# Moving the first output products of a chunk one slot later in a slot-scheduled attention and feed-forward kernel

## The chip, the cores and the metric

The kernel runs on one core of a Trainium2 chip, as one program with one launch. The metric is the time of the whole program on the device in microseconds (us). A core has five engines that run their own instruction queues in order and wait for each other on semaphores: TensorE (PE, matrix products into PSUM; PEld is its weight load), VectorE (DVE), ScalarE (ACT), GpSimd (POOL) and SyncE (SP, which here only issues DMAs).

## The reference

An attention with a 32-wide window on both sides, 512 local and 32 global positions, 8 batches and 8 heads of 64, is followed by a two-layer feed-forward with the activation h·cos(h). Cut to what matters:

```python
s_g = scale * q_g @ k_all.T;  out_g = softmax(s_g) @ v_all          # 32 global rows
s_l = concat(scale * q_l @ k_g.T, where(|i - j| <= 32, scale * q_l @ k_l.T, -1e9))
out_l = softmax(s_l) @ concat(v_g, v_l)                             # 512 local rows
x = concat(out_g, out_l) as (batch * positions, heads * 64)          # 4352 x 512
h = x @ w_in                                                        # 512 -> 2048
out = (h * cos(h)) @ w_out                                          # 2048 -> 512
```

All values are float32. The kernel gets float32 accuracy out of float16 products by splitting each operand in a high and a low part and adding three products (high·high, high·low, low·high).

## The kernel before

**Feed-forward.** The rows of x are worked off in 17 chunks of 256 rows: chunks 0 to 15 are the local rows (two chunks to a batch), chunk 16 holds the global rows of all batches. A chunk `c` has 8 steps `j`, and each step goes through these functions:

- `m1_a` (L877): 24 matmuls make the hidden tile `ph` of two 128-wide slices of the 2048. `ph` has three PSUM buffers.
- `m1_b` (L899, L900): ACT and DVE reduce the argument of the cosine (`u`).
- `m1_c` (L421): ACT takes the sine (`w`).
- `m1_d` (L912, L914, L918, L919): POOL squares `w`, DVE makes the product `gf` and so frees `ph`, ACT rounds it to `gh`, POOL makes the rest `gl`.
- `m2_a` (L933 to L935): 12 matmuls add the step to the two output tiles `po` of the chunk, six to each. `po` has two PSUM buffers, so the first `m2_a` of a chunk must wait until both tiles of the chunk before are read out.
- `m2_b` (L941, L943), after the last step: ACT reads out `po` 0 and DVE `po` 1, as tiles `o`; `m2_c` stores them.

**Attention.** Two chunks after a batch's turn its x must be ready. Each batch has four pairs of heads. For a pair: SP loads `qkr` (L432, one buffer), DVE takes its maximum `qm` (L472), makes a diagonal `d_qk` (L448), a small PE product `pm_qk` (L454) spreads the maximum over the partitions, ACT and DVE scale and split (`qa` L511, `kl` L512), PE makes four score tiles `ps` (L579, L580), DVE adds the mask and finds row minima (`t`, `mn`, L596), ACT takes the exponentials (L421), ACT and DVE write them as float16 `planes` (L673, L676), SP transposes these by DMA (L688, four for a pair) and PE multiplies with the values (`acc`, L721). Sine and exponential lie in different ACT tables, and `table_act` keeps their order as written; changing from one to the other costs an `ACT_TABLE_LOAD`.

**What sets the order.** Every call is put into a slot by `at(slot, phase, f, ...)`. Chunk `c`, step `j` has slot `8c + j` for `m1_a`; its `m2_a` lies `lag` = 3 slots later. Inside a slot the phases sort the calls: `m1_c` -9, `m1_d` -8, `m1_a` -5, `m1_b` -4, `m2_a` -3, `m2_b` -2. The slots only give the order in which the calls are written. The tile framework (`schedule_with_timeline_sim`) then simulates the program and puts the instructions of each engine in an order of its own, so a moved call can also change the order of other engines. Once written, that order is fixed: an engine whose next instruction waits does nothing else.

In a steady chunk, two pairs of heads lie beside the eight steps, one in slots 0 to 3 and one in slots 4 to 7.

Of the kernel before, what the change touches and what calls it, by code (L numbers as in the profile page):

```python
# [133 lines left out]
def body(tc, qk, v, wi, wo, mask, out):  # L134
    nc = tc.nc
    lag = 3
# [3 lines left out]
    with ExitStack() as ctx:  # L140
# [821 lines left out]
        def at(slot, phase, f, *a):  # L962
            ev[slot].append((phase, len(ev[slot]), f, a))
# [86 lines left out]
        for b in range(2, B):  # L1050
# [7 lines left out]
        ma, mb, mc, md, m2, ob, oc = (  # L1058
            (PE_, PH, PB, PD, PG2, PH2, PA0),
            (-5, -4, -9, -8, -3, -2, -10),  # L1060
            (-7, -4, -9, -8, -6, -2, -10),
        )[MF]
        for c in range(NC + 1):
            at(NS * c, -11, chunk_scales, c)
            for j in range(NS):
                s = NS * c + j
                if c == 0 and j < JS:
                    for kc in range(NPAIR):
                        at(-5 + kc, PJ, m1_a, c, j, kc)
                else:  # L1070
                    at(s, ma, m1_a, c, j)
                at(s, mb, m1_b, c, j)
                at(s + 1, mc, m1_c, c, j)
                at(s + 1, md, m1_d, c, j)
                at(s + lag, m2, m2_a, c, j)
            for k in range(CT // P):
                at(NS * c + NS - 1 + lag, ob, m2_b, c, k)
                at(NS * c + NS + lag, oc, m2_c, c, k)
# [77 lines left out]
```

## Time and profile before

| what | value |
|---|---|
| median of 3 runs | 1049.87 us (1048.74 to 1050.3) |
| the profiled execution, whole | 1045.26 us |
| its span from first to last instruction | 1043.5 us, mean granted TensorE clock 0.941 |
| PE busy in the span | 879.3 us (84%), 7819 matmuls |
| DVE / ACT / POOL busy | 729.4 (70%) / 707.9 (68%) / 463.1 us (44%) |
| PE idle before `po` L933, put down to DVE `o` L941 | 17.7 us, 11 times |
| PE idle before `ph` L877, put down to DVE `gf` L914 | 31.1 us, 12 times |

The first 250 us hold the weights' loading and splitting and the attention of the first two batches. From there to about 870 us chunks and attention run side by side, and from 870 us on the last chunks run alone. Matmuls are pipelined: each is shown longer than the step to the next one, so a busy PE is not PE at its peak. A wait is put down to the engine whose event came last.

### The profile page before, as it was taken

To read this page: it belongs to the slowest core of one execution; us is meant where nothing else is said; L and a number is where in the kernel's file an instruction comes from. 1 tells how busy PE (TensorE), PEld (TensorE's weight loads), DVE (VectorE), ACT (ScalarE), POOL (GpSimd) and SP (SyncE) were. 2 spreads that over 40 slices of the span, in tenths; PEclk is the share of its full clock that TensorE was granted. 3 is DMA by queue.
4 is the path that set the end of the run, shared out by engine and by line. 5 is a ranking of instruction groups with operands and counts; after the bars stand their busy time and mean duration, and the time that the engine had idled before them with its cause. 6 is when DMAs were issued, how large, how long until landed. Compare 5 with 4: busy or idle time off the path is not lost.

```text
span 1043.5 us, 20761 instructions
## 1 busy us (share of the span) xinstructions
PE 879.3 (84%) x7819; PEld 600.3 (58%) x7819; DVE 729.4 (70%) x1797; ACT 707.9 (68%) x1458; POOL 463.1 (44%) x396
## 2 busy tenths in 40 slices
PE   2133558677999999999899998999889999999996
PEld 1112435455566666666666666666667676666663
DVE  5997598999577777786777777877777766433231
ACT  6676478887378776877677667876777777434342
POOL 4885285957334342434233333333334333444442
PEclk9955679887999999999999999999999999999998
DMA  9869622796464546354553545455555442200000
GB/s 368 213 202 218 179 99 89 157 178 127 115 131 89 130 83 162 86 122 90 155 106 94 116 123 108 111 107 145 106 105 102 110 85 63 46 21 21 1 21 21
DMA packets 181565, 120.18 MB, mean 115 GB/s; under 512 B 159832, under 2 KB 159832, under 8 KB 179416
## 3 DMA queue, kind: packets, MB, share of 16 engines
q1 hardware_dynamic: 181464, 118.85, 47.6%
q8 instruction: 61, 1.00, 0.4%
q14 instruction: 40, 0.33, 0.1%
HBM read 51.81 MB, written 8.91 MB: 58 GB/s over the span
## 4 chain that ended last, share of the span: by engine, by line
DVE 36%; PE 29%; DMA 14%; ACT 11%; issue 6%; POOL 2%; SPq 1%; ACTq 0%; DVEq 0%; POOLq 0%
PE ph L877 12%; DMA qkr<-qk 6%; DVE t L596 5%; DVE planes L676 5%; PE po L933 5%; PE po L935 5%; PE po L934 5%; DVE u L900 4%; DMA vr<-v 3%; DVE gf L914 3%; ACT L421 3%; DVE kl L512 2%; DVE qm L472 2%; PE acc L721 2%; DVE vl L570 2%
## 5 line engine op out<-in xcount | busy, mean ns | idle before, releaser
L877 PE MATMUL ph<-xh,wi_h 128*128 128x256 f16 x1024 | 281.8, 276 | 31.1 <-DVE gf L914 31.1
L877 PE MATMUL ph<-xl,wi_h 128*128 128x256 f16 x1024 | 282.3, 276 | 0.0
L877 PE MATMUL ph<-xh,wi_l 128*128 128x256 f16 x1024 | 282.2, 276 | 0.0
L919 POOL TENSOR_TENSOR gl<-gf,gh 128x512 f16<-128x512 f32 x136 | 165.1, 1218 | 234.0 <-ACT gh L918 233.6
L912 POOL TENSOR_TENSOR w<-w 128x512 f32<-128x512 f32 x136 | 145.6, 1075 | 266.5 <-ACT w L421 254.5
L877 PEld LDWEIGHTS <-wi_h 128*128 128x128 f16 x2176 | 211.6, 99 | 68.1 <-DVE gf L914 18.4
L933 PE MATMUL po<-wo_h,gh 128*128 128x512 f16 x544 | 206.9, 384 | 21.3 <-DVE o L941 17.7
L934 PE MATMUL po<-wo_l,gh 128*128 128x512 f16 x544 | 207.2, 381 | 0.6 <-POOL wo_l L268 0.6
L935 PE MATMUL po<-wo_h,gl 128*128 128x512 f16 x544 | 206.9, 381 | 0.0
L421 ACT ACTIVATE w<-u,ca 128x512 f32<-128x512 f32 x136 | 97.0, 721 | 112.6 <-DVE u L900 112.2
L900 DVE SCALAR_TENSOR_TENSOR u<-u,cm,ph 128x512 f32<-128x512 f32 x136 | 100.0, 742 | 97.1 <-ACT u L899 97.0
L421 ACT ACTIVATE t<-t,mn 128x192 f32<-128x192 f32 (+1 forms) x256 | 117.1, 458 | 59.3 <-DVE mn L596 58.8
L918 ACT CAST gh<-gf 128x512 f16<-128x512 f32 x136 | 83.1, 611 | 78.0 <-DVE gf L914 70.6
L914 DVE SCALAR_TENSOR_TENSOR gf<-w,ph 128x512 f32<-128x512 f32 x136 | 92.5, 681 | 55.2 <-POOL w L912 55.0
L877 PEld LDWEIGHTS <-wi_l 128*128 128x128 f16 x1088 | 107.6, 99 | 15.7 <-issue 2.0
L596 DVE CUSTOM_DVE_ANT_0 t<-ps,msk,al 128x192 f32<-128x192 f32 (+1 forms) x256 | 99.5, 426 | 10.4 <-PE ps L580 10.3
L899 ACT ACTIVATE u<-ph,cm 128x512 f32<-128x512 f32 x136 | 92.1, 677 | 16.5 <-PE ph L877 16.5
L934 PEld LDWEIGHTS <-gh 128*128 128x128 f16 x544 | 53.4, 98 | 69.6 <-issue 21.2
L676 DVE SCALAR_TENSOR_TENSOR planes<-t,sm,planes 128x192 f16<-128x192 f32 (+1 forms) x192 | 83.9, 489 | 10.7 <-ACT planes L673 10.7
L935 PEld LDWEIGHTS <-gl 128*128 128x128 f16 x544 | 53.4, 98 | 64.3 <-issue 1.7
L933 PEld LDWEIGHTS <-gh 128*128 128x128 f16 x544 | 53.2, 98 | 54.0 <-issue 5.3
L421 ACT ACT_TABLE_LOAD x57 | 73.1, 1283 | 1.0
(183 smaller groups left out, 1428.4 us busy)
## 6 DMA issues: line engine op xcount, KB each, us to landing
qkr<-qk SPq DMA_DIRECT2D x29, 608.0 KB, 4.6
vr<-v SPq DMA_DIRECT2D x8, 1280.0 KB, 7.8
kh<-qa SPq DMA_DIRECT2D x62, 152.0 KB, 2.6
out<-o SPq DMA_DIRECT2D x34, 256.0 KB, 2.6
qa<-kl SPq DMA_DIRECT2D x31, 152.0 KB, 3.7
kl<-kl SPq DMA_DIRECT2D x31, 152.0 KB, 4.7
wo_h<-wi SPq DMA_DIRECT2D x4, 1024.0 KB, 7.9
raw_wi<-wi SPq DMA_DIRECT2D x4, 1024.0 KB, 10.7
```

The lines of the kernel that those rows point to most:

```text
L421: ins = nc.scalar.activation(*a, **k).ins
L596: nc.vector.tensor_tensor_reduce(t[:, h], pt[:, h], msk[:, MOFF[i] : MOFF[i] + w], al, 3.0e38, ALU.add, ALU.min, mn[:, h : h + 1],)
L676: nc.vector.scalar_tensor_tensor(lo, t[:, h], r, hi, op0=ALU.mult, op1=ALU.subtract)
L877: nc.tensor.matmul(ph[:, a], w[:, kc, f], x[:, kc, q], start=first and ip == 0, stop=last and ip == 2, skip_group_check=True,)
L899: nc.scalar.activation(u, ph, AF.Identity, bias=m)
L900: nc.vector.scalar_tensor_tensor(u, u, m, ph, op0=ALU.subtract, op1=ALU.subtract)
L912: nc.gpsimd.tensor_tensor(w, w, w, op=ALU.mult)
L914: nc.vector.scalar_tensor_tensor(gf, w, 0.5, st.pop(("ph", c, j)).rearrange("p a b -> p (a b)"), op0=ALU.subtract, op1=ALU.mult,)
L919: nc.gpsimd.tensor_tensor(gl, gf, gh, op=ALU.subtract)
L933: nc.tensor.matmul(po[k], gh[:, q], wo_h[:, f], start=(f == 0), stop=False)
L934: nc.tensor.matmul(po[k], gh[:, q], wo_l[:, f], start=False, stop=False)
L935: nc.tensor.matmul(po[k], gl[:, q], wo_h[:, f], start=False, stop=(f == NJ - 1))
```

## The change

One term is added to the slot of `m2_a`. For all chunks but the first, the products of step 0 move from slot `8c + 3` to slot `8c + 4`, where they stand behind `m1_a` of step 4 and ahead of the products of step 1.

```diff
                 at(s, mb, m1_b, c, j)
                 at(s + 1, mc, m1_c, c, j)
                 at(s + 1, md, m1_d, c, j)
-                at(s + lag, m2, m2_a, c, j)
+
+                at(s + lag + (j == 0 and c > 0), m2, m2_a, c, j)
             for k in range(CT // P):
```

No instruction is added or taken away. Names below carry chunk and step (`ph_3_4`), chunk and tile (`po_3_0`), or batch, pair and tile (`t_3_0_2`).

**PE, the turn to chunk 3, before.** Behind the last product of `ph_3_3` come the first of `po_3_0`:

```order
L877 LDWEIGHTS wi_l_87
L877 MATMUL ph_3_3_3907<-xh_1_2049,wi_l_87 128x256
L933 LDWEIGHTS gh_3_0_3691
L933 MATMUL po_3_0_3936<-wo_h_88,gh_3_0_3691 128x512
L934 LDWEIGHTS gh_3_0_3691
```

**PE, the same place now.** Behind `ph_3_3` come the 36 products of `acc_2_2`, and after them `ps`, `pm_qk` and `ph_3_4`:

```order
L877 LDWEIGHTS wi_l_87
L877 MATMUL ph_3_3_3907<-xh_1_2049,wi_l_87 128x256
L721 LDWEIGHTS vh_2_2_3208
L721 MATMUL acc_2_2_3936<-pt_2_2_3885,vh_2_2_3208 64x128
L721 LDWEIGHTS vh_2_2_3208
```

The twelve products of step 0 now follow the 24 of `ph_3_4`, with those of step 1 right behind them. The same holds for chunks 2 to 13; in chunks 14 to 16, which have no attention beside them, `ph_c_4` goes ahead of the twelve products. Chunk 1 keeps its order.

**DVE, slot 6 of chunk 3, before.** `u_3_6` comes first, then the maximum `qm_3_2` of the next pair, whose `qkr` is being loaded, then the score tile `t_3_0_2`:

```order
L914 SCALAR_TENSOR_TENSOR gf_3_5_4175<-w_3_5_4142,ph_3_5_4116 128x512
L900 SCALAR_TENSOR_TENSOR u_3_6_4204<-u_3_6_4204,cm_2_2809,ph_3_6_4179 128x512
L472 TENSOR_REDUCE qm_3_2_4337<-qkr_3_2_4239 128x1
L596 ISA t_3_0_2_4234,mn_3_0_2_4235<-ps_3_0_2_4222,msk_73,al_3_0_3576 128x224
L596 ISA mn_3_0_2_4235 128x1
```

**DVE, the same place now.** `qm_3_2` and `d_qk3_2` stand ahead of `u_3_6`:

```order
L914 SCALAR_TENSOR_TENSOR gf_3_5_4175<-w_3_5_4142,ph_3_5_4116 128x512
L472 TENSOR_REDUCE qm_3_2_4337<-qkr_3_2_4239 128x1
L448 TENSOR_SCALAR d_qk3_2_4339<-ident_64,qm_3_2_4337 128x128
L900 SCALAR_TENSOR_TENSOR u_3_6_4204<-u_3_6_4204,cm_2_2809,ph_3_6_4179 128x512
L596 ISA t_3_0_2_4234,mn_3_0_2_4235<-ps_3_0_2_4222,msk_73,al_3_0_3576 128x224
```

This happens in chunks 2, 3, 5, 7, 9 and 11. There `u_c_4` also moves ahead of `t_x_0` on DVE and `w_c_4` ahead of `u_c_5` on ACT. In chunks 4, 6, 8 and 10 `u_c_6` stays ahead of `qm`; there `u_c_4` moves ahead of `qa` on ACT and, with `gf_c_3`, ahead of `kl` on DVE, and SP issues the copy `qa<-kl` (L524) behind the pair's four transposes.

**ACT, what stands behind `u_3_6` now.** The sine `w_3_6` needs DVE's `u_3_6`; behind it come the table load, the exponentials of pair (3, 0), `gh_3_6` and `u_3_7`:

```order
L899 ACTIVATE u_3_6_4204<-ph_3_6_4179,cm_2_2809 128x512
L421 ACTIVATE w_3_6_4205<-u_3_6_4204,ca_2_2808 128x512
L421 ACT_TABLE_LOAD
L421 ACTIVATE t_3_0_0_4081,sm_3_0_4355<-t_3_0_0_4081,mn_3_0_0_4082 128x192 x2
L421 ACTIVATE t_3_0_1_4162,sm_3_0_4355<-t_3_0_1_4162,mn_3_0_1_4163 128x224 x2
L421 ACTIVATE t_3_0_2_4234,sm_3_0_4355<-t_3_0_2_4234,mn_3_0_2_4235 128x224 x2
L918 CAST gh_3_6_4242<-gf_3_6_4245 128x512
L899 ACTIVATE u_3_7_4274<-ph_3_7_4249,cm_2_2809 128x512
```

From `w_3_6` on this is also the order of before; only `gh_3_5`, which stood between `u_3_6` and `w_3_6`, has moved ahead of both.

## The prediction

> **What bounds the kernel now.** I read the waits of PE first, since the change moves PE's products, then each engine's load by stage, then the chain of waits and the timeline at one chunk's turn.
>
> ```profile
> PE po L933 <- DVE o L941: 17.1, 10, 2.7
> PE ph L877 <- DVE gf L914: 10.6, 8, 1.5
> DVE qm L472 <- DMA qkr<-qk: 41.5, 19, 3.4
> ...
> 237.00:825.00 588.00, 552.28 (x5162) 379.41 (x5159) 440.41 (x1139) 431.09 (x916) 222.97 (x195) 0.98 0.51 115
> 825.00:1043.50 218.50, 208.76 (x1655) 140.65 (x1654) 88.91 (x187) 108.13 (x201) 85.39 (x77) 0.98 0.16 35
> ```
>
> The first three are waits (us in all, times, longest): PE's from 300 to 835 us, DVE's from 310 to 800 us. The last two are busy times of PE, PEld, DVE, ACT and POOL by stage. In the steady stage PE waits 17.1 us for the read-out `o`, which is what the change aims at, and DVE waits 41.5 us for the loads of `qkr`. PE is fullest by its matmul rows (552 of 588 us), but the chain shows who sets the pace (start, us, what):
>
> ```profile
> 312.44 5.05 DMA qkr<-qk
> 317.52 1.42 DVE qm L472
> 318.94 0.36 DVE t L596
> ...
> 320.07 0.61 DVE gf L914
> ...
> 321.23 0.69 ACT u L899
> 321.94 0.75 DVE u L900
> ```
>
> A load, DVE, ACT and DVE follow each other without PE. Such loops make up nearly all of the chain from 395 to 825 us; PE stands in it only where a long wait has made it late. So **the attention's loop through the `qkr` load, DVE and ACT sets the pace up to 825 us, with PE close behind; from the last wait at 825.21 (below) PE runs without a wait and sets the end.**
>
> [...]
>
> **PE's move.** The turn to chunk 3, on DVE (two rows), then PE (two rows), with the row of `d_qk` between:
>
> ```profile
> 343.24 1.42 DVE L472 TENSOR_REDUCE qm<-qkr 128x1 f32<-128x1216 f32 x1 [1.44 <-DMA qkr<-qk]
> 344.58 0.74 DVE L941 TENSOR_SCALAR o<-po,co 128x512 f32<-128x512 f32 x1
> 345.98 0.28 DVE L448 TENSOR_SCALAR d_qk<-ident,qm 128x128 bf16<-128x128 f32 x1
> 345.37 0.38 PE L933 MATMUL po<-wo_h,gh 128*128 128x512 f16 x1 [2.02 <-DVE o L941]
> 348.39 0.22 PE L454 MATMUL pm_qk<-d_qk,ones 128*128 128x128 bf16 x1
> ```
>
> `o` is late because DVE, in order, waits for the load ahead of `qm`. PE waits until 345.37, does six `po`, 36 `acc` and four `ps`, and reaches `pm_qk` at 348.39, when `d_qk` (ended 346.26) is long there. Now `acc` and `ps` come first and PE stands at `pm_qk`, for the same DVE queue, until about 346.3: **the wait on `o` becomes a wait on `d_qk`.** Behind it come 24 `ph` and 24 `po` where there were 24 and 12. So `ph` comes 348.39 - 346.3 = 2.1 us sooner, and the end of the slot is 2.6 us (twelve `po` at 0.215) less 2.1 us, that is 0.5 us, later. In the steady stage `u_c_4` waits behind ACT's `planes` anyway, and DVE's queue to `d_qk` doesn't depend on the moved products: cost 0. Without that cover it is 0.5 us a turn. Chunk 12's turn is the last and PE's tail follows: +0.5 us.
>
> **What the swap on DVE costs.** Slot 6 of chunk 3: SP, then DVE, then ACT.
>
> ```profile
> 358.09 5.54 SPq L688 DMA_TRANSPOSE pt<-planes  x4
> 363.68 0.57 SPq L432 DMA_DIRECT2D qkr<-qk  x1
> 365.43 0.75 DVE L900 SCALAR_TENSOR_TENSOR u<-u,cm,ph 128x512 f32<-128x512 f32 x1 [0.28 <-ACT u L899]
> 368.82 1.42 DVE L472 TENSOR_REDUCE qm<-qkr 128x1 f32<-128x1216 f32 x1 [2.64 <-DMA qkr<-qk]
> 366.27 0.72 ACT L421 ACTIVATE w<-u,ca 128x512 f32<-128x512 f32 x1 [0.37 <-DVE u L900]
> 367.01 1.28 ACT L421 ACT_TABLE_LOAD   x1
> 371.81 0.62 ACT L918 CAST gh<-gf 128x512 f16<-128x512 f32 x1
> 372.33 0.68 ACT L899 ACTIVATE u<-ph,cm 128x512 f32<-128x512 f32 x1
> ...
> 343.87 0.45 ACT L421 ACTIVATE t<-t,mn 128x192 f32<-128x192 f32 x1
> 346.89 0.62 ACT L918 CAST gh<-gf 128x512 f16<-128x512 f32 x1
> ```
>
> Before, DVE does `u_3_6` at 365.43 and then idles 2.64 us for the load; meanwhile ACT takes the sine, changes tables and runs four exponentials. Now `qm` stands in front, so `u_3_6` waits for the load as well, and behind it on ACT the sine, the table load, six exponentials, `gh_3_6` and `u_3_7`. The load itself comes no sooner: SP issues it at 363.68, when four transposes that began at 358.09 are through, and the first waits for `planes0`, which follows the same work as before.
>
> From the start of `qm` to ACT's `u_3_7` it was 372.33 - 368.82 = 3.51 us. Now: `qm` 1.34 (343.24 to 344.58), `d_qk` 0.28, `u` 0.75, sine 0.74 (366.27 to 367.01), table load 1.30, six exponentials with nothing late 3.02 (343.87 to 346.89), `gh` 0.52 (371.81 to 372.33), in all 7.95 us. The difference is **4.4 us**. Nothing behind it takes this up: `u_3_7`, `t_3_0_3`, the next exponentials and sine follow on each other, and the next load of `qkr` hangs on them. `acc` and `xh` are not later than that. The swap is made in chunks 2, 3, 5, 7, 9 and 11; the last reads alike:
>
> ```profile
> 797.79 1.42 DVE L472 TENSOR_REDUCE qm<-qkr 128x1 f32<-128x1216 f32 x1 [2.63 <-DMA qkr<-qk]
> 801.31 0.68 ACT L899 ACTIVATE u<-ph,cm 128x512 f32<-128x512 f32 x1
> ```
>
> 3.52 us again. Six times 4.4 is **+26.4 us**. The trace doesn't show this order, so the bounds are 0 a turn (the load comes before `u_c_6`) and 5.0 (all of `u`'s delay, from 365.43 to 370.44, passes on); I take 4.4, built from rows.
>
> **What comes back.** At three turns DVE's `t` waited for PE's `ps`, which lay behind `po`:
>
> ```profile
> 296.76 0.42 DVE L596 CUSTOM_DVE_ANT_0 t<-ps,msk,al 128x192 f32<-128x192 f32 x1 [1.81 <-PE ps L580]
> 563.40 0.42 DVE L596 CUSTOM_DVE_ANT_0 t<-ps,msk,al 128x192 f32<-128x192 f32 x1 [1.34 <-PE ps L580]
> 777.78 0.42 DVE L596 CUSTOM_DVE_ANT_0 t<-ps,msk,al 128x192 f32<-128x192 f32 x1 [1.27 <-PE ps L580]
> ```
>
> `ps` now lies ahead of `po`: **-4.4 us**.
>
> **Chunks 4, 6, 8 and 10.** `u_c_4` ahead of `qa` delays ACT by 0.6 us.
>
> ```profile
> 409.97 1.36 SPq L803 DMA_TRANSPOSE ptg<-planes_g  x1
> 412.59 5.49 SPq L688 DMA_TRANSPOSE pt<-planes  x4
> ```
>
> DVE does `u_c_4` and `gf_c_3` while it would wait for `qa`, so `planes0` comes no later, the transposes may start some 0.5 us sooner, and the copy L524, now behind them, uses that up ahead of the `qkr` load. PE's 10.6 us of waits for `gf` mostly go, but PE then stands at `pm_qk`. I take 0, within 0.5 us each; uncovered, the 0.6 us would pass on.
>
> **The clock.** PE's longer idling has a price of its own:
>
> ```profile
> 502.81 0.38 PE L933 MATMUL po<-wo_h,gh 128*128 128x512 f16 x1 [2.21 <-DVE o L941]
> ...
> 558.57 0.38 PE L933 MATMUL po<-wo_h,gh 128*128 128x512 f16 x1 [2.50 <-DVE o L941]
> ...
> 559.46 0.63 PE L933 MATMUL po<-wo_h,gh 128*128 128x512 f16 x1
> 559.89 0.63 PE L934 MATMUL po<-wo_l,gh 128*128 128x512 f16 x1
> ...
> 346.83 1.29 PE acc L721 x36
> ...
> 560.95 1.98 PE acc L721 x36
> ...
> 825.21 0.38 PE L933 MATMUL po<-wo_h,gh 128*128 128x512 f16 x1 [1.07 <-DVE o L941]
> ```
>
> After 2.50 us of idling products follow each other at 0.43 us instead of 0.215, and `acc` takes 1.98 instead of 1.29 us: about 1.7 us lost (five `po` at 0.215, and 0.69). After 2.21 us it isn't seen. With DVE 4.4 us later at chunk 11, PE idles longer than 2.5 us before chunk 12's tail, so it pays 1.7 us once on the path. At earlier turns PE has room, as DVE and ACT come later still.
>
> [...]
>
> **Sum**: 26.4 - 4.4 + 0.5 + 1.7 = +24.2 us. On the profiled execution's 1045.26 us that is 1069.5; that execution is 4.6 us below the median of the runs, 1049.87, to which I add the same: **1074.0 us**.
>
> **Rivals.**
> - *PE is the bound* (matmul rows at 94% speak for it, the chain against): the 17.1 us go, 1032.8 us. Decided by whether PE waits at `pm_qk`. 5%.
> - *The load comes in time.* If `qkr` lands before `u_c_6` is ready (365.4 us at chunk 3), the swap costs nothing: 1049.87 - 4.4 + 0.5 = 1046.0. It would have to land 2.6 us sooner or more (DVE's wait in the row at 368.82); SP's transposes speak against it. 6%. This is the case on the other side.
> - *The stall is taken up*, because PE's `acc` and not ACT held `u_c_7` (the chain runs through `acc` at chunk 3): cost and gains cancel, 1050. Six near-equal distances of 3.5 us speak against it. 4%.
> - *The clock falls on the path at every turn*: at the ten turns from chunk 3 to 12, nine more times 1.7 us, 1089 us. PE's room speaks against it. 5%.
>
> **How the numbers follow.** 80% for the forecast. The range is 1056 to 1086: the low end is half of each stall covered, on the profiled execution's time (1045.3 + 13.2 - 4.4 + 2.2), the high end is the stall at 5.0, no gain back, and three turns at the low clock (1049.9 + 30.0 + 0.5 + 5.1 = 1085.5). That leaves out the first three rivals and the last. Faster by over 0.2% (2.1 us, about what a measurement can tell) 11%, within it 4%, slower 85%.
>
> **What would show it.** Right: PE's wait on `o` gone and a wait of `pm_qk` on `d_qk` in its place; six times about 3.5 us of DVE idling ahead of `qm` directly behind `gf_c_5`; about 8 us from `qm` to `u_c_7` at those six turns and 3.5 at the others; chunk 12's turn 20 us or more later than 825. Wrong: loads that land before `u_c_6`, or turns no further apart than before although DVE stalls.

## The result and the profile after

The changed kernel takes **1072.31 us** (median of 4 runs, 1071.65 to 1073.62) against 1049.3 us for the kernel before (4 runs): ratio 1.0224, 95% interval 1.0203 to 1.0246, so 23.0 us slower. Its profiled execution took 1072.69 us with a span of 1070.9 us. Two executions far off the rest, one of 4433.6 us of qm_last below (with it, the median would be 1036.68 us) and one of 1575.72 us of the kernel before, are left out of the medians and ratios.

The waits of PE from 300 to 855 us in the changed kernel (us in all, times, longest):

```profile
PE pm_qk L454 <- DVE d_qk L448: 24.0, 10, 3.5
PE ph L877 <- ACT xh L745: 7.6, 5, 1.9
PE ps L579 <- DVE mn L596: 3.8, 7, 1.5
```

No wait on `o` is left in this stretch. Ten waits of `pm_qk` stand in its place, and they are longer than what they replace.

The busy times by stage, cut at the turn to chunk 12 (window, us, busy PE, PEld, DVE, ACT and POOL; then granted clock of PE, DMA share and GB/s):

```profile
237.00:850.00 613.00, 560.97 (x5211) 383.22 (x5212) 446.81 (x1145) 430.76 (x918) 224.52 (x196) 0.98 0.49 111
850.00:1070.90 220.90, 209.62 (x1621) 140.38 (x1620) 89.85 (x188) 108.22 (x203) 85.34 (x77) 0.98 0.15 35
```

The steady stage is 25 us longer, the tail 2.4 us. The chain of waits of the changed kernel, at slot 6 of chunk 5 (start, us, what):

```profile
478.51 5.10 DMA qkr<-qk
...
483.64 1.43 DVE qm L472
...
485.09 0.29 DVE d_qk L448
485.38 0.67 DVE u L900
...
486.13 0.72 ACT w L421
486.87 1.28 ACT L421
488.17 0.58 ACT t L421 x3
...
488.96 2.05 ACT t L421 x9
491.01 0.51 ACT gh L918
491.52 0.59 ACT u L899
```

This is the stall that the prediction drew: load, `qm`, `d_qk`, then `u_5_6`, its sine, the table load, the exponentials, `gh` and `u_5_7`, one behind the other.

The time from one turn to the next (between the starts of DVE's `o`) shows where the difference lies. Swapped turns are those of the chunks in which `qm` and `d_qk` went ahead of `u_c_6`:

| chunk | 2 | 3 | 4 | 5 | 6 | 7 | 8 | 9 | 10 | 11 |
|---|---|---|---|---|---|---|---|---|---|---|
| swapped | yes | yes | no | yes | no | yes | no | yes | no | yes |
| before, us | 55.14 | 50.75 | 54.65 | 52.04 | 55.75 | 52.87 | 55.46 | 50.38 | 55.74 | 52.20 |
| changed, us | 57.02 | 55.93 | 54.24 | 56.28 | 56.37 | 56.50 | 54.95 | 55.14 | 56.16 | 56.41 |

The six swapped chunks give +23.9 us, the four others +0.1. The stretch behind chunk 12's turn is 1.8 us longer (220.9 against 219.1), and 1.6 us lie ahead of chunk 2. Together that is the 27.4 us between the two spans. The orders of the two kernels differ only from chunk 2 on, and the first turn comes anywhere from 257.3 to 263.9 us in the traces of all runs, so the 1.6 us belong to the spread between executions.

### The profile page after: what moved, and what is told of

It is laid out like the page before. It is cut to its first block, busy times and chain, and to the rows that moved or that the text cites. A ratio compares the mean times of both kernels' runs of the same rounds, so it can differ in the third digit from the quotient of the medians.

```text
span 1070.9 us, 20771 instructions
## 1 busy us (share of the span) xinstructions
PE 887.6 (83%) x7819; PEld 602.8 (56%) x7819; DVE 736.4 (69%) x1797; ACT 705.0 (66%) x1458; POOL 462.5 (43%) x396
## 4 chain that ended last, share of the span: by engine, by line
DVE 35%; PE 24%; ACT 16%; DMA 12%; issue 8%; POOL 3%; SPq 1%; ACTq 0%; DVEq 0%; POOLq 0%
PE ph L877 10%; DMA qkr<-qk 5%; DVE planes L676 5%; DVE u L900 5%; DVE t L596 4%; ACT t L421 4%; PE po L933 4%; PE po L935 4%; PE po L934 4%; ACT L421 4%; DVE gf L914 2%; DVE kl L512 2%; DMA vr<-v 2%; ACT w L421 2%; ACT u L899 2%
## 5 line engine op out<-in xcount | busy, mean ns | idle before, releaser
L877 PE MATMUL ph<-xh,wi_h 128*128 128x256 f16 x1024 | 286.1, 280 | 28.1 <-DVE gf L914 20.5
L877 PE MATMUL ph<-xl,wi_h 128*128 128x256 f16 x1024 | 286.4, 280 | 1.9 <-DVE xl L746 1.9
L877 PE MATMUL ph<-xh,wi_l 128*128 128x256 f16 x1024 | 286.6, 280 | 0.0
L877 PEld LDWEIGHTS <-wi_h 128*128 128x128 f16 x2176 | 214.6, 100 | 87.1 <-issue 39.7
L676 DVE SCALAR_TENSOR_TENSOR planes<-t,sm,planes 128x192 f16<-128x192 f32 (+1 forms) x192 | 91.7, 532 | 10.8 <-ACT planes L673 10.8
L579 PE MATMUL ps<-kh,qa 128*128 128x192 f16 (+1 forms) x256 | 60.3, 271 | 16.5 <-DVE mn L596 9.6
```

Of the source, the lines that this page charges most:

```text
L676: nc.vector.scalar_tensor_tensor(lo, t[:, h], r, hi, op0=ALU.mult, op1=ALU.subtract)
L877: nc.tensor.matmul(ph[:, a], w[:, kc, f], x[:, kc, q], start=first and ip == 0, stop=last and ip == 2, skip_group_check=True,)
```

## The experiments

Each time is a median beside runs of the kernel before on the same chip (medians 1048.2 to 1048.7 us). Line numbers shift by a few between the kernels.

| run | us | ratio to before, 95% interval |
|---|---|---|
| u_first | 1054.84 | 1.0055 (1.0027 to 1.0083) |
| swap_alone | 1072.77 | 1.0244 (1.0195 to 1.0294) |
| load_early | 1057.44 | 1.0086 (1.0062 to 1.0110) |
| load_early_u_first | 1051.20 | 1.0047 (1.0022 to 1.0073) |
| pe_alone | 1046.81 | 0.9982 (0.9961 to 1.0004) |
| others_alone | 1078.06 | 1.0277 (1.0228 to 1.0326) |
| u4_even | 1047.18 | 0.9988 (0.9969 to 1.0008) |
| w4_odd | 1052.53 | 1.0046 (1.0024 to 1.0069) |
| pe_and_swap | 1074.20 | 1.0254 (1.0229 to 1.0278) |
| qm_last | 1034.32 | 0.9886 (0.9838 to 0.9934) |
| qm_last_pe_moved | 1036.43 | 0.9891 (0.9845 to 0.9938) |
| vm_last_too | 1019.30 | 0.9718 (0.9685 to 0.9750) |

### The swap, undone and alone

**u_first** binds `qm` behind `u_c_6` in the changed kernel:

```diff
+                c = 2 * b - 4 + p // 2
+                if b > 2 and p % 2 == 0 and True:
+                    tc.add_manual_dep(qi, st["ui", c, 6].name, order, reason="u_first")
```

> The changed kernel (1072.31 us) with one thing undone: at the six turns DVE does u_c_6 ahead of qm and d_qk again; PE's, ACT's, POOL's and SP's orders stay those of the changed kernel. Theory (the swap costs 4.4 us at each of six turns, the rest of the change brings 4.4 and costs 0.5 to 2): 1072.3 - 26.4 = 1046 us, between 1043 and 1049, with 3.5 us from qm to ACT's u_c_7 at all turns. Rival (PE's moved products, or the other moves on ACT, DVE and SP, cost the time and the swap only stands beside them): above 1060 us.

1054.84 us: 17.5 us come back, less than expected (the range ended at 1049), and the kernel stays 0.55% above before. Something else in the change costs time once the swap is gone.

**swap_alone** makes the swap in the kernel before (`m1_b2` is the DVE half of `m1_b`, bound behind `d_qk`):

```diff
+            if b > 2 and p % 2 == 0 and 2 * b - 4 + p // 2 in SWAP:
+                at(o["qa"] - 1, PJ + 0.5, qk_a, b, p)
...
+                if c in SWAP and j == 6:
+                    at(s, PJ + 0.6, m1_b2, c, j)
```

> The kernel before (1049.3 us) with the swap alone: at the same six turns qm and d_qk stand ahead of u_c_6 on DVE; PE's, POOL's and SP's orders are those of before, and on ACT only gh_c_6 and u_c_7 change places. Theory: 1049.3 + 6 x 4.4 = 1076 us, between 1069 and 1080; a little above the changed kernel, since PE's waits for ps at three turns stay. Rival (the swap costs only together with PE's move): within 5 us of 1049.

1072.77 us, 24.3 above before and inside the expected range: the swap alone makes nearly all of the loss, without PE's move.

### The load

**load_early** keeps the order of PE, DVE, ACT and POOL of the changed kernel and lets SP issue the load earlier. The swap is bound by hand for this, as in swap_alone; SP's copy L524 goes behind the transposes. The line that moves the load:

```diff
-            at(o["load"], PJ, load_qk, b, p)
+            at(o["load"], PA0 if b > 2 and p % 2 == 0 else PJ, load_qk, b, p)
```

> The changed kernel with the swap kept (the orders of PE, DVE, ACT and POOL are the same), but SP issues the qkr load of every second pair (p 0 and 2 of batches 3 to 7) ahead of the four transposes instead of behind them; the copy L524 goes behind the transposes. The load should land about 5 us sooner, some 366 us at the turn where qm began at 372.54, and DVE should do qm directly behind gf_c_5. Theory (the swap costs because u_c_6 waits for the load): the stall falls from about 3.5 us to 0.5 a turn, so at least 6 x 2.7 = 16 us come back: 1056 us or less, down to about 1040 if the loop through the load gets shorter at the other turns too. Rival (the order on DVE and ACT itself costs 4.4 us, load or not): 1068 to 1072. A second rival (the transposes, now later by the load, hold acc): 1072 or more.

DVE in this kernel, slot 6 of chunk 5:

```profile
474.09 0.69 DVE L929 SCALAR_TENSOR_TENSOR gf<-w,ph 128x512 f32<-128x512 f32 x1 [0.63 <-POOL w L927]
474.70 1.41 DVE L474 TENSOR_REDUCE qm<-qkr 128x1 f32<-128x1216 f32 x1
476.14 0.60 DVE L449 TENSOR_SCALAR d_qk<-ident,qm 128x128 bf16<-128x128 f32 x1
476.67 0.73 DVE L912 SCALAR_TENSOR_TENSOR u<-u,cm,ph 128x512 f32<-128x512 f32 x1
```

`qm` follows `gf_5_5` with no idle time, in the same order that cost 3.1 us of idling here in the changed kernel. The time is 1057.44 us, 1.4 us above the range that was expected: 14.9 us came back, so the order without the late load costs little. What stays is the remainder that u_first showed too.

**load_early_u_first** makes both edits.

> Both edits at once: the load ahead of the transposes, and u_c_6 ahead of qm. Theory: the swap's price is the wait for the load, so beside load_early this gains only 0 to 4 us (the u behind qm and d_qk costs under 0.7 us a turn where the load is there); and if the loop through the load sets the pace up to 825 us, an earlier load makes this one faster than u_first: 1033 to 1044, where PE becomes the bound at about 1033. Rival (the load's place matters only through the swap): the time of u_first, within 2 us.

1051.20 us, 3.6 below u_first. Both expectations failed: the time did not fall towards 1033, and it is not u_first's either. The earlier load took away the waits in the middle of the chunks, but DVE still waits ten times at the turns (16.3 us for `qkr` from 300 to 830 us, 27.2 in u_first). Its longest waits here are those for ACT's `u`: 63.7 us, against 32.1 in the kernel before. So in this order ACT is late too; why, the runs w4_odd and u4_even below look into.

### The two halves of the change

From here on the order of an engine is written out: at the end of the kernel every instruction of that engine is bound behind its forerunner in a list, so that nothing else moves.

```diff
+            for x, y in zip(seq, seq[1:]):
+                tc.add_manual_dep(v[y], v[x].name, order, reason="pin")
```

**pe_alone** takes PE's order from the changed kernel and all other orders from before.

> PE in the order of the changed kernel, every other engine (DVE, ACT, POOL, SP) in the order of before, all written out by hand. By the prediction's steps the PE move itself costs 0.5 us once and frees 4.4 us at the three turns where t waited for ps: 1049 - 3.9 = about 1045 us. Rival (the 0.5 us is not covered and is paid at each of the ten turns, and what is freed is lost again): 1052 to 1056, the time of u_first (1054.8). Second rival (the moves of u_c_4 and w_c_4 on ACT and DVE cost what u_first has over before): 1045 to 1050.

**others_alone** takes PE's order from before and all others from the changed kernel.

> The other half: PE in the order of before, every other engine in the order of the changed kernel. Theory (the time is lost by the orders on DVE and ACT): the swap's 24.3 us as in swap_alone and 3 to 7 us for the moves of u_c_4 and w_c_4, 1074 to 1081 us, at or above the changed kernel. Rival (the loss needs PE's move): 1049 to 1060.

1046.81 and 1078.06 us. PE's move alone is worth -1.9 us (-4.1 to +0.4). The reordering of the other engines, which the scheduler added, is worth +29 us alone; beside it PE's move takes 5.7 us back by the medians (1078.06 to 1072.31; the two intervals overlap). The waits of PE in pe_alone, 300 to 855 us:

```profile
PE pm_qk L457 <- DVE d_qk L451: 18.8, 10, 3.6
PE ph L880 <- DVE gf L917: 8.1, 7, 1.5
PE gps L765 <- DVE gmn L782: 1.2, 3, 0.5
```

PE now waits about as long for `d_qk` as it did for `o` before (18.8 and 17.1 us): the move only renames the wait.

### What else the scheduler moved

**u4_even** puts only the moves in chunks 4, 6, 8 and 10 on top of pe_alone (ACT's part):

```diff
+ACTIVATE u_4_4<-ph_4_4,cm_4 128x512
 ACTIVATE qa_3_3<-qkr_3_3,qs_3_3 128x1216
...
+ACTIVATE w_4_4<-u_4_4,ca_4 128x512
-ACTIVATE u_4_4<-ph_4_4,cm_4 128x512
 CAST gh_4_3<-gf_4_3 128x512
 ACTIVATE u_4_5<-ph_4_5,cm_4 128x512
-ACTIVATE w_4_4<-u_4_4,ca_4 128x512
```

> pe_alone (1046.8 us) with the changed kernel's orders on DVE, ACT, POOL and SP in chunks 4, 6, 8 and 10 only: u_c_4 ahead of qa on ACT, u_c_4 and gf_c_3 behind kl on DVE, the copy L524 behind the transposes. The prediction took these for 0. Theory (u_c_4's 0.57 us on ACT delays qa and nothing covers it, with up to as much again behind it): 4 x 0.6 to 4 x 1.1, so 1049 to 1051 us. Rival (covered, as predicted): within 1.5 us of 1046.8.

**w4_odd** puts only those in chunks 2, 3, 5, 7, 9 and 11 on top, without the swap (ACT's part):

```diff
+ACTIVATE w_5_4<-u_5_4,ca_4 128x512
 ACTIVATE u_5_5<-ph_5_5,cm_4 128x512
-ACTIVATE w_5_4<-u_5_4,ca_4 128x512
 ACTIVATE w_5_5<-u_5_5,ca_4 128x512
...
+CAST gh_5_5<-gf_5_5 128x512
 ACTIVATE u_5_6<-ph_5_6,cm_4 128x512
-CAST gh_5_5<-gf_5_5 128x512
```

> pe_alone with the changed kernel's orders on DVE and ACT in chunks 2, 3, 5, 7, 9 and 11 only, but u_c_6 ahead of qm as before: t_x_0 behind u_c_4 on DVE, w_c_4 ahead of u_c_5 and gh_c_5 ahead of u_c_6 on ACT. The prediction gave this no price. Theory (u_c_5 and u_c_6 come 2.6 to 4.6 us later, the sines and the table load behind them too, and ACT's exponentials end 0.7 to 1.0 us later): 6 x 0.7 to 6 x 1.0, so 1051 to 1053 us. Rival (covered): within 1.5 us of 1046.8, and the 5.8 us of u_first lie elsewhere.

u4_even is within 0.4 us of pe_alone, so the run's own expectation (1049 to 1051 us) failed: in these chunks all of it is covered, as the prediction had said, though `w_c_4` goes ahead of `u_c_5` here too. w4_odd costs 5.7 us, as expected. It makes several moves at once; the share of `w_c_4` alone was not measured, and the rows below are what speaks for it. ACT in chunk 5, first pe_alone, then w4_odd:

```profile
464.14 0.68 ACT L902 ACTIVATE u<-ph,cm 128x512 f32<-128x512 f32 x1
467.68 1.38 ACT L424 ACTIVATE w<-u,ca 128x512 f32<-128x512 f32 x2 [2.86 <-DVE u L903]
...
472.36 0.72 ACT L424 ACTIVATE w<-u,ca 128x512 f32<-128x512 f32 x1 [0.37 <-DVE u L903]
473.10 1.28 ACT L424 ACT_TABLE_LOAD   x1
...
476.87 0.48 ACT L424 ACTIVATE t<-t,mn 128x224 f32<-128x224 f32 x1 [0.56 <-DVE mn L599]
```

```profile
471.90 0.72 ACT L424 ACTIVATE w<-u,ca 128x512 f32<-128x512 f32 x1 [3.45 <-DVE u L903]
472.52 0.67 ACT L902 ACTIVATE u<-ph,cm 128x512 f32<-128x512 f32 x1
474.07 0.72 ACT L424 ACTIVATE w<-u,ca 128x512 f32<-128x512 f32 x1 [0.88 <-DVE u L903]
...
478.74 0.72 ACT L424 ACTIVATE w<-u,ca 128x512 f32<-128x512 f32 x1 [0.87 <-DVE u L903]
479.48 1.28 ACT L424 ACT_TABLE_LOAD   x1
...
483.06 0.47 ACT L424 ACTIVATE t<-t,mn 128x224 f32<-128x224 f32 x1
```

In pe_alone `u_5_5` is done long before the sines, which then run as a pair (x2). In w4_odd it stands behind the first sine, so each sine waits for its own trip through DVE. From the first sine to the table load it is 5.4 us (467.68 to 473.10) in the one and 7.6 us (471.90 to 479.48) in the other. In pe_alone the last exponentials wait 0.56 us for DVE. In w4_odd they wait for nothing: ACT itself is late, by 1.1 us at `gh_5_6` as counted from the turn.

**pe_and_swap** has the swap on top of pe_alone and none of these moves:

```diff
 SCALAR_TENSOR_TENSOR gf_3_5<-w_3_5,ph_3_5 128x512
-SCALAR_TENSOR_TENSOR u_3_6<-u_3_6,cm_2,ph_3_6 128x512
 TENSOR_REDUCE qm_3_2<-qkr_3_2 128x1
+TENSOR_SCALAR d_qk3_2<-ident,qm_3_2 128x128
+SCALAR_TENSOR_TENSOR u_3_6<-u_3_6,cm_2,ph_3_6 128x512
```

> pe_alone (1046.8 us) with the swap alone on top: at the six turns DVE does qm and d_qk ahead of u_c_6; the other moves of u_c_4, w_c_4, gh_c_5 and L524 stay undone. It settles why the swap costs 24 us in swap_alone but only 17.5 us between u_first and the changed kernel. Theory (the swap and the move of w_c_4 delay the same exponentials, so the later of the two alone counts): the swap's full price, 1046.8 + 24.3 = 1071 us, within 1.5 us of the changed kernel. Rival (the prices add, and the swap is worth 17.5 us under PE's moved order): 1064.3 us.

1074.20 us, 1.9 us above the changed kernel (1.5 were expected) and not 8 us below it: 27.4 us above pe_alone. So the prices of the swap and of `w_c_4` do not add. DVE in chunk 5, first pe_and_swap, then the changed kernel:

```profile
480.58 0.69 DVE L917 SCALAR_TENSOR_TENSOR gf<-w,ph 128x512 f32<-128x512 f32 x1 [0.31 <-POOL w L915]
485.41 1.42 DVE L475 TENSOR_REDUCE qm<-qkr 128x1 f32<-128x1216 f32 x1 [4.15 <-DMA qkr<-qk]
```

```profile
479.84 0.69 DVE L914 SCALAR_TENSOR_TENSOR gf<-w,ph 128x512 f32<-128x512 f32 x1 [0.63 <-POOL w L912]
483.64 1.42 DVE L472 TENSOR_REDUCE qm<-qkr 128x1 f32<-128x1216 f32 x1 [3.11 <-DMA qkr<-qk]
```

With `w_c_4` early, `gf_5_5` ends 1.3 us later as counted from the turn (DVE's `o`), and DVE idles 1.0 us less ahead of the load (3.11 against 4.15). So `qm` begins only 0.2 us later, and what follows it is the same: 7.78 us to `u_5_7` in both. The delay of `w_c_4` is spent inside the stall.

### The other way round

**qm_last** is the kernel before with DVE's order turned round at the twenty places where `qm` waits: `t_x_2`, and at a chunk's turn `o` as well, go ahead of it.

```diff
-TENSOR_REDUCE qm_3_3<-qkr_3_3 128x1
 TENSOR_SCALAR o_3_1<-po_3_1,co_2 128x512
 ISA t_3_1_2,mn_3_1_2<-ps_3_1_2,msk,al_3_1 128x224
...
+TENSOR_REDUCE qm_3_3<-qkr_3_3 128x1
 TENSOR_SCALAR d_qk3_3<-ident,qm_3_3 128x128
```

> The kernel before with DVE's order changed the other way round: at the twenty places where DVE waits for a load of qkr, what is ready goes ahead of qm instead of behind it (t_x_2 at the middle of a chunk, o and t_x_2 at its turn); all other engines keep their order. Theory (in-order DVE loses what stands behind the wait): at each place up to 0.7 to 1.4 us come sooner, 20 x 0.7 = 14 to 20 x 1.4 = 28 us, bounded by PE's waits of 28 us from 300 to 835: 1022 to 1036, and PE's wait for o goes from 17 us to near 0. Rival (the load itself sets the pace, and DVE's work behind it was hidden beside ACT): within 4 us of 1049.

**qm_last_pe_moved** has the same DVE order under PE's order of the changed kernel.

> The same DVE order under PE's order of the changed kernel. With o ahead of the load, the moved products have nothing left to avoid, and pm_qk, which still hangs on the load, now stands ahead of them. Theory: slower than qm_last by 0.5 us a turn or more, 3 to 10 us. Rival (PE's place doesn't matter since DVE sets the pace): within 2 us of qm_last.

1034.32 and 1036.43 us. The first is 1.1% faster than before and inside the expected range, near its upper end. PE no longer waits for `o` from 300 to 815 us. The second expectation failed: PE's place makes no difference that the runs can tell (ratios 0.9886 and 0.9891). The turns of chunks 3, 5, 7, 9 and 11 fell to 49.6 to 50.5 us, those of 4, 6, 8 and 10 stayed at 53.9 to 56.0, and the DVE timeline of qm_last shows why:

```profile
504.89 2.82 DVE L543 TENSOR_REDUCE vm<-vr 128x1 f32<-128x2560 f32 x1 [3.23 <-DMA vr<-v]
507.62 0.74 DVE L903 SCALAR_TENSOR_TENSOR u<-u,cm,ph 128x512 f32<-128x512 f32 x1
```

It is the same pattern with another load: `u_6_3` waits for nothing of its own, and stands behind `vm`, which waits for the values of the next batch.

**vm_last_too** moves `vm` of these four chunks as well:

```diff
-TENSOR_REDUCE vm_4<-vr_4 128x1
 SCALAR_TENSOR_TENSOR u_4_3<-u_4_3,cm_4,ph_4_3 128x512
...
+TENSOR_REDUCE vm_4<-vr_4 128x1
 SCALAR_TENSOR_TENSOR kl_3_3<-qkr_3_3,qs_3_3,qa_3_3 128x1216
```

> qm_last (1036.7 us) with one more move on DVE: in chunks 4, 6, 8 and 10 vm, which waits 3.2 us for the load of vr and then takes 2.7 us, goes from ahead of u_c_3 to directly ahead of kl, where DVE waits 1.7 us for qa anyway. PE, ACT, POOL and SP keep the order of before. Theory (the even turns of 54 to 56 us are set by that wait, the odd ones of 50 us by PE): each even turn falls by 3.2 + 2.7 - 1.1 = 4.8 us at most, to PE's 50: 4 x 4 to 4 x 4.8, so 1017 to 1021 us. Rival (another wait takes its place): 1030 us or more.

1019.30 us, as expected: **2.8% faster than before** (0.9718, 0.9685 to 0.9750). From chunk 3 to chunk 11 all turns are 49.6 to 51.3 us. Its busy times up to the turn to chunk 12, and all of PE's waits from 300 to 790 us:

```profile
237.00:799.00 562.00, 549.03 (x5176) 378.03 (x5176) 440.34 (x1150) 429.26 (x918) 223.59 (x195) 0.99 0.54 120
```

```profile
PE ph L880 <- DVE gf L917: 4.4, 7, 0.8
PE pm_qk L457 <- DVE d_qk L451: 0.6, 1, 0.6
PE gps L765 <- DVE gmn L782: 0.5, 1, 0.5
```

PE waits 5.5 us in 490: now it is the bound. The weight loads are 378 of 562 us (67%), hardly more than the 65% of before (379 of 588); the matmul rows (98% against 94%) tell this state better.

## Why the prediction was right

The forecast was 1074.0 us, measured were 1072.31. By its steps:

- **PE's move.** The wait on `o` became a wait of `pm_qk` on `d_qk`, at ten turns, as forecast. Alone it is worth -1.9 us (-4.1 to +0.4). The forecast for it and the stalls it frees, +0.5 - 4.4 = -3.9 us, lies near the edge of that interval. By the turns of the traces the three chunks with these stalls (2, 7 and 11) are together 4.3 us shorter in pe_alone than before, as forecast, and the seven others together 1.75 us longer. In the changed kernel these three grew by 3.2 us on average, and the other three swapped chunks by 4.7. The idle time of DVE's `t` that is put down to PE's `ps` fell from 10.3 to 3.5 us over the whole run (its group on the page).
- **The swap.** 26.4 us were forecast for six turns, 27.4 us are measured on top of pe_alone and 24.3 on the kernel before (20.4 to 30.8). From `qm` to ACT's `u_c_7` the trace has 7.78 to 7.99 us at the six turns (forecast 7.95). DVE idles 2.7 to 3.3 us ahead of `qm` there (forecast about 3.5). In the middle of chunks 4, 6, 8 and 10 it is 3.8 to 5.0 us from `qm` to `u_c_7`, where the prediction had named 3.5.
- **Chunks 4, 6, 8 and 10.** Forecast 0, measured +0.1 us in the trace and +0.4 us in u4_even.
- **The clock at the tail.** 2.2 us (1.7 and 0.5) were forecast, 1.8 measured. PE at the turn to chunk 12:

```profile
851.77 0.27 PE L454 MATMUL pm_qk<-d_qk,ones 128*128 128x128 bf16 x1 [3.18 <-DVE d_qk L448]
851.83 0.42 PE L877 MATMUL ph<-xh,wi_h 128*128 128x256 f16 x1
852.04 0.42 PE L877 MATMUL ph<-xl,wi_h 128*128 128x256 f16 x1
...
854.53 0.27 PE L877 MATMUL ph<-xl,wi_h 128*128 128x256 f16 x1
854.64 0.27 PE L877 MATMUL ph<-xh,wi_l 128*128 128x256 f16 x1
```

Twelve `ph` follow each other at 0.21 us instead of 0.11 (the granted clock was 0.50 from 851.03 to 854.44), which is 1.25 us. The rest is the 0.5 us of the longer slot: in u4_even, which has PE's order of pe_alone and begins chunk 12 at full rate (`ph` every 0.11 us), it takes 46.57 us against 46.06 before. But the reason given for the step (it pays because it idles over 2.5 us) does not hold, as the last section shows, and what brought the half rate to the tail was not shown: chunk 12 takes 47.85 us in the changed kernel and 48.23 in w4_odd, which both meet it there, after 3.18 and 2.90 us of idling.

- **The offset.** The forecast added 4.6 us because the profiled execution of before lay that far below its median. That of the changed kernel lies 0.4 us above its own. The sum has to be held against the 23.0 us between the medians (24.2 forecast), not against the 27.4 us between the spans.
- **What had no price.** The move of `w_c_4` ahead of `u_c_5` was listed as part of the change and not counted. With what goes with it, it costs 5.7 us without the swap and nothing beside it, so the sum was right although a step was missing. That was luck: nothing in the prediction says that the stall would take it up. The expectation of 1046 us for u_first, made from the same steps, failed by 9 us mostly for this reason; what makes up the rest was not measured.

The rivals fall: in the changed kernel PE waits at `pm_qk`, so it is not the bound; the load comes after `u_c_6` is ready; nothing takes the stall up; and the half rate, seen at four of the ten turns from chunk 3 to 12 (granted clock 0.50), left no clear mark on the path before chunk 12: chunks 6 and 8, which begin with it, changed by +0.6 and -0.5 us. Chunk 11 begins with it as well (+4.2 us), but is a swapped one, and the two can't be told apart there.

## What to carry to other kernels

On an in-order engine, the price of an instruction that waits is what stands ready behind it (24.3 us for the six turns of swap_alone); so read which loads an engine idles for, and put everything that is ready ahead of them. When a change moves one engine's work, compare the order of all engines: here the scheduler's answer on DVE cost 27 us, and the move that was asked for made no measurable difference. Prices of two delays on one path do not add where the first ends in a wait for something that comes at its own time (`w_c_4` early, with what goes with it, cost 5.7 us without the swap and nothing beside it), so test a sum with the parts alone and together.

## What the runs showed of the hardware

In these runs the clock's half rate does not follow from the length of an idle spell. The prediction had read a limit between 2.21 and 2.50 us from the trace of before. PE in pe_and_swap at the turn to chunk 11, then in the changed kernel in chunk 9:

```profile
796.86 0.22 PE L457 MATMUL pm_qk<-d_qk,ones 128*128 128x128 bf16 x1 [3.02 <-DVE d_qk L451]
796.92 0.27 PE L880 MATMUL ph<-xh,wi_h 128*128 128x256 f16 x1
797.03 0.27 PE L880 MATMUL ph<-xl,wi_h 128*128 128x256 f16 x1
```

```profile
716.03 0.27 PE L877 MATMUL ph<-xh,wi_h 128*128 128x256 f16 x1 [1.65 <-ACT xh L745]
...
717.77 0.28 PE L877 MATMUL ph<-xl,wi_h 128*128 128x256 f16 x1 [0.37 <-DVE xl L746]
717.88 0.38 PE L877 MATMUL ph<-xh,wi_l 128*128 128x256 f16 x1
718.06 0.42 PE L877 MATMUL ph<-xh,wi_h 128*128 128x256 f16 x1
```

After 3.02 us of idling the products go on at full rate, every 0.11 us. After 1.65, 0.29 and 0.37 us, with eight products between, they fall to half rate, every 0.21 us.

The granted clock shows the same (window, us, busy PE, PEld, DVE, ACT and POOL, granted clock, DMA share, GB/s), first the changed kernel, then pe_and_swap:

```profile
714.50:717.91 3.41, 1.22 (x10) 0.85 (x10) 2.46 (x9) 2.81 (x8) 1.15 (x1) 1.00 0.00 0
717.91:721.33 3.42, 3.42 (x22) 1.91 (x20) 2.11 (x12) 3.41 (x8) 1.04 (x1) 0.50 0.00 0
```

```profile
794.89:798.31 3.42, 1.45 (x14) 1.30 (x14) 2.52 (x8) 3.29 (x13) 0.18 (x1) 1.00 0.41 122
798.31:801.72 3.41, 3.41 (x24) 2.10 (x23) 2.99 (x14) 2.82 (x9) 0.98 (x1) 1.00 0.00 0
```

In the changed kernel it was 1.00 from 714.50 to 717.91 us and 0.50 from there to 721.33. In pe_and_swap it was 1.00 in both windows, the first of which holds the end of the 3.02 us. What brings the half rate on was not shown.
